# Batch 0 of linear attention and a low-rank mixer: q's tail used last, A on 32 rows, the second heads' k.v amid the normalisations

## The chip, the cores and the metric

One core of a Trainium2 chip runs the whole program. The metric is device time in microseconds (us) of one execution. Seven runs of the kernel before gave a median of 320.61 us (319.73 to 321.92).

## The reference

Eight batches; each has q, k and v with 8 heads of 576 rows by 64. Attention is linear: relu, each row weighted once by a cosine and once by a sine of its position, and no softmax.

```python
def phi(x, c, s):
    r = np.maximum(x, 0.0)
    return np.concatenate([r * c, r * s], axis=-1)
q_p, k_p = phi(q, cos_w, sin_w), phi(k, cos_w, sin_w)
kv = np.einsum('bhsf,bhsd->bhfd', k_p, v)
z = np.sum(k_p, axis=2)
num = np.einsum('bhsf,bhfd->bhsd', q_p, kv)
den = np.einsum('bhsf,bhf->bhs', q_p, z)[..., None] + 1e-06
x = num / den                        # heads side by side: 576 x 512 per batch
h = x.transpose(0, 2, 1) @ U @ V     # U: 576 x 32, V: 32 x 576
u = x + h.transpose(0, 2, 1)
out = u + np.maximum(u @ w_ch1, 0.0) @ w_ch2   # 512 -> 2048 -> 512
```

## The kernel before

**Tiling.** A batch's 576 rows are four blocks of 128 rows ("main", loaded as one 1 MB transfer) and a tail of 64 (one transfer of 128 KB in pieces of 256 bytes). The tails of two batches share a tile of 128 rows: batch 0 has rows 0 to 63 of it, batch 1 rows 64 to 127. All products are in bf16 with sums in f32.

**Stages of a batch.** `q_prep`, `k_prep` and `v_prep`/`v_block` turn loads into bf16 tiles (relu times cosine on VectorE, times sine on ScalarE, a cast for v, which has a column of ones beside each head so that k.v also yields z). `qtr_unit` transposes a block of q on TensorE and has VectorE or ScalarE copy it to `q_pT`, or to `q_tlT` for the tail. `kv_unit` is k.v for four heads (20 products, L271), `den_unit` the 20 products for the denominators (L330) with two VectorE operations for the reciprocals (L322, L323), `xh_unit` four products per block (L347) and their normalisation on VectorE (L351). `A_unit` (L392) makes A = U^T x, 32 by 512. `uTd_open` writes x transposed into PSUM (L444), `uTd_mm` adds A and V to it (L458), and `uTd_evac` copies it as uT. `u_unit` (L409) makes u untransposed. `g1_main` is the hidden layer (4 products of 512 columns for each of 16 blocks, L493, and a relu on ScalarE, L502), `g2_part` the output layer (L545).

**A in four parts.** In the kernel before, the five blocks of rows in `A_unit` go to four column groups of 32 (`lo = c % 4 * R`): blocks 0 to 3 each to its own, the tail on top of group 0. A thus stands as four partial sums on 128 rows, and V is needed four times one below the other. `V_four` makes this `V_bf` out of the loaded `V_32` with two products against four identities (L199, L203), and `V_evac` copies it on ScalarE.

**Order of the work.** The instructions of each engine run in the order in which the Python code calls them (`manual_schedule`); the framework adds the waits. PSUM tiles are drawn from rotating sets named X, T (one buffer each), o (two) and g (three), so an operation can also wait for the reader of an older tile. For batches 2 to 7 a plan places attention beside the hidden layer of earlier batches. Batches 0 and 1 are written out by hand. Batch 0 has nothing beside it: `keep_warm` puts filler products (L179) on TensorE. After the front (q blocks, their transposes, k blocks; L706 to L715) `chain_head(0)` takes v's first heads, k.v of heads 0 to 3, their denominators and normalisations, and k.v of heads 4 to 7 after the fourth block. `chain_mid(0)` does the other four heads, opens two of the four transposed blocks, makes the first half of A and closes the two blocks; `chain_end(0)` makes the second half of A and opens the other two blocks. Then `g1_main` of batch 0 starts, with batch 1's transposes between its blocks. Batch 1 runs through `chain_head(1)`, `chain_mid(1)` and `chain_end(1)` in the same way, with `g1_main` of batch 0 as filling.

**Loads.** SP issues the loads of q, k and v (`load_main` L75, `load_tail` L81) in program order, for batch 0: q, q tail, k, k tail, v tail, v's first four heads, v's other heads; then V and U, then batch 1. qst, qt, vst and vt have one buffer each, so that a load of batch 1 waits for the readers of batch 0. GpSimd issues the weights: the first block of w1 (`w1_load(0)`, 512 columns) behind a copy that waits for batch 0's k tail (L717), the second behind its cast of V, the other two behind batch 1's transposed q tail (L755), w2 later.

Of the kernel before, what the change touches and what calls it, by code (L numbers as in the profile page):

```python
# [17 lines left out]
def kernel(  # L18
# [58 lines left out]
            in_=src[b, h0:h1, 0:512, :].rearrange("h (p c) d -> p h (c d)", c=4),  # L77
        )

    def load_tail(dst, src, b, eng=None):  # L80
        (eng or nc.sync).dma_start(  # L81
            out=dst[tail(b), :, :],
            in_=src[b, :, 512:S, :].rearrange("h s d -> s h d"),
        )

    w1_bf = const.tile([P, 4, DH], BF16)
# [37 lines left out]
            allow_small_or_imprecise_dtypes=True,  # L124
        )
    load_main(qst[0], q, 0)
    load_tail(qt[0], q, 0)
    load_main(kst[0], k, 0)
    load_tail(kt[0], k, 0)
    load_tail(vt[0], v, 0)  # L130
    load_main(vst[0], v, 0, 0, 4)
    load_main(vst[0], v, 0, 4, 8)
    nc.sync.dma_start(out=stV, in_=moe_V)
    nc.sync.dma_start(
# [250 lines left out]
    def A_unit(b, tag, bufs, eng=None, n0=0, n1=DM, a_ps=None):  # L385
        if b not in A_sb:
            A_sb[b] = pool.tile([P, DM], BF16, tag="A_sb", bufs=2, name="A_sb")
        if a_ps is None:
            a_ps = ps.tile([P, DM], FP32, tag=tag, bufs=bufs, name="a_ps")
        for c in range(5):  # L390
            lo = c % 4 * R
            nc.tensor.matmul(  # L392
                out=a_ps[lo : lo + R, n0:n1],
                lhsT=U_of(b, c),
                rhs=x_of(b, c)[:, n0:n1],
                start=(c < 4),
                stop=(c > 0),
            )
        cast(eng or V_, A_sb[b][:, n0:n1], a_ps[:, n0:n1])
        return a_ps  # L400

    def u_unit(b, c, tag, bufs):
        if b not in u_bf:
            u_bf[b] = pool.tile([P, 4, DM], BF16, tag="u_bf", bufs=3, name="u_bf")
            if b % 2 == 0:
                u_tl[b // 2] = pool.tile([P, DM], BF16, tag="u_tl", bufs=2, name="u_tl")
        rows = slice(0, P) if c < 4 else tail(b)
        va = ps.tile([P, DM], FP32, tag=tag, bufs=bufs, name="va_ps")
        nc.tensor.matmul(out=va, lhsT=V_bf[:, c, :], rhs=A_sb[b], start=True, stop=True)  # L409
        nc.vector.tensor_tensor(  # L410
            out=u_bf[b][:, c, :] if c < 4 else u_tl[b // 2][rows, :],
            in0=x_of(b, c, rows),
            in1=va[rows, :],
            op=ALU.add,
        )
# [40 lines left out]
    def uTd_mm(b, d):  # L456
        t = uT_ps[b, d]
        nc.tensor.matmul(  # L458
            out=t.rearrange("m c t -> m (c t)"), lhsT=A_sb[b][:, d * P : d * P + P],
            rhs=V_bf[:, 0:4, :].rearrange("r c t -> r (c t)"), start=False, stop=True,  # L460
        )

    def uTt_direct(pr, tag, bufs, eng):
        uTt_alloc(pr)
        t = ps.tile([P, 4, P], FP32, tag=tag, bufs=bufs, name="uTt_ps")
        for d in range(4):
            dd = slice(d * P, d * P + P)
            nc.tensor.matmul(
                out=t[:, d, :], lhsT=x_tl[:, dd], rhs=ident, start=(d == 0), stop=False
            )  # L470
            for i in range(2):
                nc.tensor.matmul(
                    out=t[:, d, tail(i)], lhsT=A_sb[2 * pr + i][:, dd],
                    rhs=V_bf[:, 4, tail(i)], start=False, stop=(d == 3 and i == 1),
                )
        cast(eng, uT_tl[pr], t)

# [93 lines left out]
    def loads(b, eng):  # L571
        def kk():
            alloc_k(b)
            load_tail(kt[b], k, b, eng)
            load_main(kst[b], k, b, eng=eng)

        def vv():
            alloc_v(b)
            load_tail(vt[b], v, b, eng)
            load_main(vst[b], v, b, eng=eng)  # L580

        def qq():
            alloc_q(b)
            load_tail(qt[b], q, b, eng)
            load_main(qst[b], q, b, eng=eng)

        return kk, vv, qq
# [58 lines left out]
    TL = (0, 1, 2, 3, 4)  # L646
    O2, G3 = ("o", 2), ("g", 3)

    def chain_head(b, fill, xt):
        if b == 0:  # L650
            v_prep(b, 0, 4, (4,), (A_,))
            v_block(b, 0, 4, 0, 3, V_)
            v_block(b, 0, 4, 3, 4, A_)
        kv_unit(b, 0, "T", 1)
        fill(0)
        rec0 = den_unit(b, 0, 4, "X", 1)
        if b == 0:
            v_prep(b, 4, 8, (4,), (A_,))
        v_block(b, 4, 8, 0, 4, A_)
        fill(1)  # L660
        for n, c in enumerate(ORD):
            xh_unit(b, c, 0, 4, rec0, *xt[n])
            if n == 1:
                fill(2)
            if n == 3:
                kv_unit(b, 1, "T", 1, A_)
        if b == 0:
            V_four("X", 1)
            V_evac(A_)

    def chain_mid(b, fill, xt, dt):
        fill(3)
        m = 3 if b == 0 else 2
        rec1 = den_unit(b, 4, 8, *dt)
        if b == 1:

            nc.sync.dma_start(out=mark2, in_=rec1[0:1, 0, 0:1])
        for n, c in enumerate(ORD[:m]):
            xh_unit(b, c, 4, 8, rec1, *xt[n])
        u01 = ps.tile([P, 2, 512], FP32, tag="X", bufs=1, name="u01")  # L680
        uTd_open(b, 0, None, None, u01[:, 0, :].rearrange("p (c t) -> p c t", c=4))
        uTd_open(b, 1, None, None, u01[:, 1, :].rearrange("p (c t) -> p c t", c=4))
        a0 = A_unit(b, "T", 1, A_, 0, 256)
        for n in (m, m + 1):
            xh_unit(b, ORD[n], 4, 8, rec1, *xt[n])
        fill(4)
        uTd_mm(b, 0)
        uTd_mm(b, 1)
        uTd_evac(b, 0, A_)
        uTd_evac(b, 1, V_ if b == 0 else A_)  # L690
        for n in range(m + 2, 5):
            xh_unit(b, ORD[n], 4, 8, rec1, *xt[n])
        fill(5)
        return a0

    def chain_end(b, a0):
        A_unit(b, "T", 1, V_, 256, 512, a0)
        uTd_open(b, 2, "o", 2)
        uTd_open(b, 3, "o", 2)

    def warm0(n):
        m = (2, 1, 0, 1, 1, 2)[n]
        if m:
            keep_warm(m, *(O2 if n == 0 else G3))

# [54 lines left out]
    st1 = {}  # L760
# [7 lines left out]
    xt1 = (O2, O2, O2, O2, O2)  # L768
    at(7, lambda: keep_warm(2, "X", 1))
    at(7, lambda: chain_head(1, fill1, xt1))  # L770
    at(7, lambda: st1.update(a=chain_mid(1, fill1, xt1, ("T", 1))))
    at(7, lambda: chain_end(1, st1["a"]))
    at(13, lambda: uTd_close(1, 2, V_), lambda: uTd_close(1, 3, A_))

    slots, todo = [], {}
# [59 lines left out]
```

## Time and profile before

| | |
|---|---|
| median of 7 runs | 320.61 us (319.73 to 321.92) |
| the profiled execution: its time, its span from first to last instruction | 321.55 us, 319.6 us |
| TensorE busy | 311.8 us, 98% of the span |
| VectorE, ScalarE, GpSimd busy | 154.2, 150.4, 34.8 us |
| mean granted clock of TensorE | 0.995 |
| moved by DMA | 51.90 MB, 162 GB/s over the span |
| filler products (L179) | 42, 12.9 us |
| first hidden product of batch 0 (L493) | starts at 22.58 us |
| k.v of batch 1 in full flow (L271) | from 35.28 us |

All times within the execution are counted from the start of the span. A row of a timeline gives start and length, engine, line, operation, output and inputs, the number of instructions merged into the row, and in brackets how long the engine had been idle before it and what ended that. PE is TensorE, PEld its weight loads, ACT ScalarE, DVE VectorE, POOL GpSimd, SP the engine that issues loads. A busy TensorE is not always doing useful work: in the first 22 us much of it is filler. A row's start is the safe reading; a product is shown with its whole pipeline time, so that rows of TensorE overlap.

### The profile page before, as it was taken

Reading aid. Unit: us, or ns where it says so; the run is one execution under the profiler, and the core shown is the slowest. Engines: PE = TensorE matmul, PEld = TensorE weight load, DVE = VectorE, ACT = ScalarE, POOL = GpSimd, SP = SyncE. Lnnn points to the kernel's source line nnn. Section 1 sums busy time; section 2 is a strip of 40 time slices with the busy share of each in tenths; the row PEclk is TensorE's granted clock in tenths of the full one; section 3 lists DMA queues with packets and bytes.
Section 4 is the critical chain, followed back from the end, with each engine's and each line's share of the span. In section 5 each row is a group of like instructions: output and inputs, shape, how many; then the busy total and the mean of one; then the engine's idle time right before and its main releaser. Section 6 shows DMA issues by size and latency. Waiting matters only on the chain.

```text
span 319.6 us, 5781 instructions
## 1 busy us (share of the span) xinstructions
PE 311.8 (98%) x2386; PEld 162.8 (51%) x2386; DVE 154.2 (48%) x341; ACT 150.4 (47%) x251; POOL 34.8 (11%) x71
## 2 busy tenths in 40 slices
PE   8899799999999999999999999999999999999996
PEld 3565464475545544475455444565454444464443
DVE  5777653762777646036926585154836520001211
ACT  3857655585904256658500077558400166750000
POOL 2232500200120140000211100000121100000000
PEclk9999799999999999999999999999999999999999
DMA  7999999987198937990799859930692140001122
GB/s 216 297 259 267 209 211 299 281 236 238 36 202 164 292 101 141 227 281 12 163 197 284 279 116 180 295 120 21 134 211 71 60 98 0 2 0 68 66 83 81
DMA packets 83755, 51.90 MB, mean 162 GB/s; under 512 B 51890, under 2 KB 80946, under 8 KB 83730
## 3 DMA queue, kind: packets, MB, share of 16 engines
q1 hardware_dynamic: 77154, 40.21, 52.7%
q0 software_dynamic: 6432, 11.27, 14.6%
q8 instruction: 18, 0.29, 0.4%
q10 hardware_dynamic: 144, 0.07, 0.1%
q14 instruction: 7, 0.06, 0.1%
HBM read 36.86 MB, written 9.44 MB: 145 GB/s over the span
## 4 chain that ended last, share of the span: by engine, by line
PE 87%; DMA 7%; SPq 2%; ACT 1%; DVE 1%; issue 0%; DVEq 0%
PE o_ps L545 39%; PE g_ps L493 33%; DMA kt<-in_k_dram 5%; PE gt_ps L513 4%; PE kv_ps L271 3%; PE va_ps L409 3%; PE x_ps L365 3%; DMA vst<-in_v_dram 2%; SPq L81 1%; PE a_ps L392 1%; ACT k_p L237 1%; PE t_ps L288 1%; SPq L75 1%; ACT hid L502 0%; PE xh_ps L347 0%
## 5 line engine op out<-in xcount | busy, mean ns | idle before, releaser
L502 ACT ACTIVATE hid<-g_ps 128x512 bf16<-128x512 f32 x128 | 76.3, 597 | 102.4 <-PE g_ps L493 101.9
L493 PE MATMUL g_ps<-uT,w_bf 128*128 128x512 bf16 x512 | 119.7, 382 | 0.4 <-DMA w_bf<-in_moe_w_ch_dram 0.4
L545 PE MATMUL o_ps<-w_bf,hid 128*128 128x512 bf16 (+2 forms) x528 | 119.2, 373 | 0.0
L493 PEld LDWEIGHTS <-w_bf 128*128 128x128 bf16 x512 | 49.0, 98 | 56.9 <-issue 1.4
L545 PEld LDWEIGHTS <-hid 128*128 128x128 bf16 x528 | 48.7, 98 | 52.8 <-issue 1.7
L555 DVE TENSOR_TENSOR o_sb<-u_bf,o_ps 128x512 f32<-128x512 bf16 (+2 forms) x33 | 22.1, 670 | 62.7 <-PE o_ps L545 62.6
L565 POOL DMA_DIRECT2D out_dram<-o_sb x24 | 13.5, 563 | 164.4 <-DVE o_sb L555 154.4
L410 DVE TENSOR_TENSOR u_bf<-x_bf,va_ps 128x512 bf16<-128x512 bf16 x32 | 21.8, 687 | 10.1 <-PE va_ps L409 10.1
L105 DVE CAST kv<-kv_ps 128x260 bf16<-128x260 f32 x14 | 6.0, 429 | 32.2 <-PE kv_ps L271 32.2
L237 ACT ACTIVATE q_p<-qst,sinw 128x512 bf16<-128x512 f32 x22 | 15.1, 713 | 4.7 <-DMA qst<-in_q_dram 4.7
L375 DVE TENSOR_TENSOR x_bf<-x_ps,rec 128x512 bf16<-128x512 f32 x24 | 16.6, 691 | 0.8
L513 PE MATMUL gt_ps<-uT_tl,w_bf 128*128 128x128 bf16 x256 | 15.6, 219 | 0.0
L409 PE MATMUL va_ps<-A_sb,V_bf 128*128 128x512 bf16 x40 | 15.2, 379 | 0.0
L545 PE MATMUL o_ps<-w_bf,hid_tl 128*128 128x512 bf16 x64 | 15.1, 379 | 0.0
L513 PEld LDWEIGHTS <-w_bf 128*128 128x128 bf16 x256 | 14.6, 98 | 0.5
L322 DVE TENSOR_SCALAR rec<-x_ps 128x8 f32<-128x8 f32 (+1 forms) x30 | 5.0, 165 | 20.2 <-PE x_ps L365 20.1
L179 PE MATMUL w_ps<-zero 128*128 128x512 bf16 x42 | 12.9, 442 | 1.8 <-DVE halfpi L142 1.2
L271 PEld LDWEIGHTS <-k_p 128*128 128x128 bf16 x256 | 11.3, 97 | 5.5 <-ACT k_p L237 2.0
L271 PE MATMUL kv_ps<-v_ext,k_p 128*128 128x65 bf16 x256 | 12.2, 193 | 1.5 <-ACT k_p L237 0.8
L239 DVE TENSOR_SCALAR k_p<-kst,cosw 128x512 bf16<-128x512 f32 x27 | 13.0, 499 | 0.0
L103 ACT ACTIVATE v_ext<-vst 128x512 bf16<-128x512 f32 (+2 forms) x19 | 12.3, 661 | 0.9 <-DMA vst<-in_v_dram 0.8
L520 ACT ACTIVATE hid_tl<-gt_ps 128x512 bf16<-128x512 f32 x16 | 9.4, 598 | 5.5 <-PE gt_ps L513 5.5
(105 smaller groups left out, 249.7 us busy)
## 6 DMA issues: line engine op xcount, KB each, us to landing
qst<-in_q_dram SPq DMA_DIRECT2D x8, 1024.0 KB, 10.4
kst<-in_k_dram SPq DMA_DIRECT2D x8, 1024.0 KB, 7.8
vst<-in_v_dram SPq DMA_DIRECT2D x6, 1024.0 KB, 10.3
out_dram<-o_sb POOLq DMA_DIRECT2D x24, 256.0 KB, 4.5
w_bf<-in_moe_w_ch_dram POOLq DMA_DIRECT2D x8, 512.0 KB, 10.8
vst<-in_v_dram SPq DMA_DIRECT2D x4, 512.0 KB, 8.3
out_dram<-o_sb SPq DMA_DIRECT2D x7, 256.0 KB, 2.3
qt<-in_q_dram SPq DMA_DIRECT2D x8, 128.0 KB, 9.2
```

The source lines that it names most:

```text
L237: nc.scalar.activation(out=o, in_=i, func=AF.Relu, bias=0.0, scale=w)
L239: eng.tensor_scalar(out=o, in0=i, scalar1=0.0, scalar2=w, op0=ALU.max, op1=ALU.mult)
L271: nc.tensor.matmul(out=acc[:, i, :], lhsT=k_p[b][:, c, h, :] if c < 4 else k_tl[:, h, :], rhs=vx[:, c, h, :], start=(c == 0), stop=(c == 4),)
L375: nc.vector.tensor_tensor(out=x_of(b, c, rows).rearrange("p (g i d) -> p g i d", g=2, d=D), in0=view[:, :, :, 0:D], in1=rec[rows].unsqueez ...
L409: nc.tensor.matmul(out=va, lhsT=V_bf[:, c, :], rhs=A_sb[b], start=True, stop=True)
L410: nc.vector.tensor_tensor(out=u_bf[b][:, c, :] if c < 4 else u_tl[b // 2][rows, :], in0=x_of(b, c, rows), in1=va[rows, :], op=ALU.add,)
L493: nc.tensor.matmul(out=g_ps.rearrange("p (c t) -> p c t", c=4), lhsT=w1_bf[:, d, j * P : j * P + P], rhs=uT[b][:, :, d, :], start=(d == 0) ...
L502: nc.scalar.activation(out=hid[b][:, j, :], in_=g_ps, func=AF.Relu, bias=0.0, scale=1.0)
L513: nc.tensor.matmul(out=g_ps[:, jj, :], lhsT=w1_bf[:, d, j * P : j * P + P], rhs=uT_tl[pr][:, d, :], start=(d == 0), stop=(d == 3),)
L545: nc.tensor.matmul(out=o[:, cols], lhsT=lhs[:, j, c * P : c * P + P], rhs=w2_bf[:, j, cols], start=(j == 0), stop=(j == NJ - 1),)
L555: nc.vector.tensor_tensor(out=o_sb[:, cols], in0=u[:, cols], in1=o[:, cols], op=ALU.add)
L565: eng.dma_start(out=out[b, 0:512, cols].rearrange("(p c) n -> p c n", c=4)[:, c, :], in_=o_sb[:, cols],)
```

## The change

It concerns batch 0 and, by moved names alone, batch 1, whose calls keep their order.

- **Loads.** q's tail of batch 0 is issued behind k, its tail, the first four heads of v's tail (a transfer of its own now) and the first half of v. The rest of v's tail follows it, then v's second half. There is one transfer more.
- **q's tail used last.** `q_prep` and `qtr_unit` of the tail stand after v's first casts, and around the first k.v, instead of before k. The blocks are normalised in the order 0, 1, 2, 3, tail.
- **Second heads' k.v** comes after the second block of the first normalisations instead of the fourth, and the first denominators are now called after the casts of v's second heads.
- **A on 32 rows.** For batch 0 all five products add up in one group of 32 rows, A's copies take 32 rows, and whatever uses A of batch 0 takes `V_32`. `V_four` and `V_evac` stay for the other batches.
- **Around A.** For batch 0 the first half of A goes ahead of the opening of the first two transposed blocks, and ScalarE copies both. The denominators of the second heads use the set T.
- **Fillers.** Five products of `keep_warm` fewer.
- The loads of batch 1 are written down behind the whole of batch 0's chain; SP issues them in the same order as before.

```diff
@@ -77,10 +77,10 @@
             in_=src[b, h0:h1, 0:512, :].rearrange("h (p c) d -> p h (c d)", c=4),
         )
 
-    def load_tail(dst, src, b, eng=None):
+    def load_tail(dst, src, b, h0=0, h1=H, eng=None):
         (eng or nc.sync).dma_start(
-            out=dst[tail(b), :, :],
-            in_=src[b, :, 512:S, :].rearrange("h s d -> s h d"),
+            out=dst[tail(b), h0:h1, :],
+            in_=src[b, h0:h1, 512:S, :].rearrange("h s d -> s h d"),
         )
 
     w1_bf = const.tile([P, 4, DH], BF16)
@@ -124,11 +124,12 @@
             allow_small_or_imprecise_dtypes=True,
         )
     load_main(qst[0], q, 0)
-    load_tail(qt[0], q, 0)
     load_main(kst[0], k, 0)
     load_tail(kt[0], k, 0)
-    load_tail(vt[0], v, 0)
+    load_tail(vt[0], v, 0, 0, 4)
     load_main(vst[0], v, 0, 0, 4)
+    load_tail(qt[0], q, 0)
+    load_tail(vt[0], v, 0, 4, 8)
     load_main(vst[0], v, 0, 4, 8)
     nc.sync.dma_start(out=stV, in_=moe_V)
     nc.sync.dma_start(
@@ -388,16 +389,25 @@
         if a_ps is None:
             a_ps = ps.tile([P, DM], FP32, tag=tag, bufs=bufs, name="a_ps")
         for c in range(5):
-            lo = c % 4 * R
+            lo = c % 4 * R if b > 0 else 0
             nc.tensor.matmul(
                 out=a_ps[lo : lo + R, n0:n1],
                 lhsT=U_of(b, c),
                 rhs=x_of(b, c)[:, n0:n1],
-                start=(c < 4),
-                stop=(c > 0),
-            )
-        cast(eng or V_, A_sb[b][:, n0:n1], a_ps[:, n0:n1])
+                start=(c < 4) if b > 0 else (c == 0),
+                stop=(c > 0) if b > 0 else (c == 4),
+            )
+        rows = slice(0, P) if b > 0 else slice(0, R)
+        cast(eng or V_, A_sb[b][rows, n0:n1], a_ps[rows, n0:n1])
         return a_ps
+
+
+
+    def A_of(b, cols=slice(0, DM)):
+        return A_sb[b][:, cols] if b > 0 else A_sb[b][0:R, cols]
+
+    def V_of(b):
+        return V_bf if b > 0 else V_32
 
     def u_unit(b, c, tag, bufs):
         if b not in u_bf:
@@ -406,7 +416,7 @@
                 u_tl[b // 2] = pool.tile([P, DM], BF16, tag="u_tl", bufs=2, name="u_tl")
         rows = slice(0, P) if c < 4 else tail(b)
         va = ps.tile([P, DM], FP32, tag=tag, bufs=bufs, name="va_ps")
-        nc.tensor.matmul(out=va, lhsT=V_bf[:, c, :], rhs=A_sb[b], start=True, stop=True)
+        nc.tensor.matmul(out=va, lhsT=V_of(b)[:, c, :], rhs=A_of(b), start=True, stop=True)
         nc.vector.tensor_tensor(
             out=u_bf[b][:, c, :] if c < 4 else u_tl[b // 2][rows, :],
             in0=x_of(b, c, rows),
@@ -456,8 +466,8 @@
     def uTd_mm(b, d):
         t = uT_ps[b, d]
         nc.tensor.matmul(
-            out=t.rearrange("m c t -> m (c t)"), lhsT=A_sb[b][:, d * P : d * P + P],
-            rhs=V_bf[:, 0:4, :].rearrange("r c t -> r (c t)"), start=False, stop=True,
+            out=t.rearrange("m c t -> m (c t)"), lhsT=A_of(b, slice(d * P, d * P + P)),
+            rhs=V_of(b)[:, 0:4, :].rearrange("r c t -> r (c t)"), start=False, stop=True,
         )
 
     def uTt_direct(pr, tag, bufs, eng):
...
@@ -646,69 +656,84 @@
     TL = (0, 1, 2, 3, 4)
     O2, G3 = ("o", 2), ("g", 3)
 
-    def chain_head(b, fill, xt):
-        if b == 0:
-            v_prep(b, 0, 4, (4,), (A_,))
-            v_block(b, 0, 4, 0, 3, V_)
-            v_block(b, 0, 4, 3, 4, A_)
-        kv_unit(b, 0, "T", 1)
-        fill(0)
-        rec0 = den_unit(b, 0, 4, "X", 1)
-        if b == 0:
-            v_prep(b, 4, 8, (4,), (A_,))
-        v_block(b, 4, 8, 0, 4, A_)
-        fill(1)
-        for n, c in enumerate(ORD):
-            xh_unit(b, c, 0, 4, rec0, *xt[n])
-            if n == 1:
-                fill(2)
-            if n == 3:
-                kv_unit(b, 1, "T", 1, A_)
-        if b == 0:
-            V_four("X", 1)
-            V_evac(A_)
-
-    def chain_mid(b, fill, xt, dt):
-        fill(3)
-        m = 3 if b == 0 else 2
-        rec1 = den_unit(b, 4, 8, *dt)
-        if b == 1:
-
-            nc.sync.dma_start(out=mark2, in_=rec1[0:1, 0, 0:1])
-        for n, c in enumerate(ORD[:m]):
-            xh_unit(b, c, 4, 8, rec1, *xt[n])
+    def chain_begin(b):
         u01 = ps.tile([P, 2, 512], FP32, tag="X", bufs=1, name="u01")
-        uTd_open(b, 0, None, None, u01[:, 0, :].rearrange("p (c t) -> p c t", c=4))
-        uTd_open(b, 1, None, None, u01[:, 1, :].rearrange("p (c t) -> p c t", c=4))
-        a0 = A_unit(b, "T", 1, A_, 0, 256)
-        for n in (m, m + 1):
-            xh_unit(b, ORD[n], 4, 8, rec1, *xt[n])
-        fill(4)
-        uTd_mm(b, 0)
-        uTd_mm(b, 1)
-        uTd_evac(b, 0, A_)
-        uTd_evac(b, 1, V_ if b == 0 else A_)
-        for n in range(m + 2, 5):
-            xh_unit(b, ORD[n], 4, 8, rec1, *xt[n])
-        fill(5)
-        return a0
+        for d in (0, 1):
+            uTd_open(b, d, None, None, u01[:, d, :].rearrange("p (c t) -> p c t", c=4))
 
     def chain_end(b, a0):
         A_unit(b, "T", 1, V_, 256, 512, a0)
         uTd_open(b, 2, "o", 2)
         uTd_open(b, 3, "o", 2)
 
-    def warm0(n):
-        m = (2, 1, 0, 1, 1, 2)[n]
-        if m:
-            keep_warm(m, *(O2 if n == 0 else G3))
+    def chain0():
+        v_prep(0, 0, 4, (4,), (A_,))
+        v_block(0, 0, 4, 0, 3, V_)
+        v_block(0, 0, 4, 3, 4, A_)
+        q_prep(0, 4, (V_, A_))
+        kv_unit(0, 0, "T", 1)
+        qtr_unit(0, 4, 0, H, V_, *G3)
+        v_prep(0, 4, 8, (4,), (A_,))
+        v_block(0, 4, 8, 0, 4, A_)
+        rec0 = den_unit(0, 0, 4, "X", 1)
+        for n, c in enumerate(TL):
+            xh_unit(0, c, 0, 4, rec0, *(O2, O2, G3, G3, G3)[n])
+            if n == 1:
+                kv_unit(0, 1, "T", 1, A_)
+        V_four("X", 1)
+        V_evac(A_)
+        rec1 = den_unit(0, 4, 8, "T", 1)
+        for n, c in enumerate(TL[:3]):
+            xh_unit(0, c, 4, 8, rec1, *(O2, O2, G3)[n])
+        a0 = A_unit(0, "T", 1, A_, 0, 256)
+        chain_begin(0)
+        for n, c in enumerate(TL[3:]):
+            xh_unit(0, c, 4, 8, rec1, *G3)
+        keep_warm(1, "o", 2)
+        uTd_mm(0, 0)
+        uTd_mm(0, 1)
+        uTd_evac(0, 0, A_)
+        uTd_evac(0, 1, A_)
+        keep_warm(1, "o", 2)
+        return a0
+
+    def chain1(fill):
+        kv_unit(1, 0, "T", 1)
+        fill(0)
+        rec0 = den_unit(1, 0, 4, "X", 1)
+        v_block(1, 4, 8, 0, 4, A_)
+        fill(1)
+        for n, c in enumerate(ORD):
+            xh_unit(1, c, 0, 4, rec0, *O2)
+            if n == 1:
+                fill(2)
+            if n == 3:
+                kv_unit(1, 1, "T", 1, A_)
+        fill(3)
+        rec1 = den_unit(1, 4, 8, "T", 1)
+
+        nc.sync.dma_start(out=mark2, in_=rec1[0:1, 0, 0:1])
+        for n, c in enumerate(ORD[:2]):
+            xh_unit(1, c, 4, 8, rec1, *O2)
+        chain_begin(1)
+        a0 = A_unit(1, "T", 1, A_, 0, 256)
+        for c in ORD[2:4]:
+            xh_unit(1, c, 4, 8, rec1, *O2)
+        fill(4)
+        uTd_mm(1, 0)
+        uTd_mm(1, 1)
+        uTd_evac(1, 0, A_)
+        uTd_evac(1, 1, A_)
+        xh_unit(1, ORD[4], 4, 8, rec1, *O2)
+        fill(5)
+        chain_end(1, a0)
 
     keep_warm(18, "X", 1)
-    for c in TL:
+    for c in TL[:4]:
         q_prep(0, c, (V_, V_ if c == 3 else A_))
-    for n, c in enumerate(TL):
-        qtr_unit(0, c, 0, H, (V_, A_, V_, A_, V_)[n], *(G3 if n < 3 else O2))
-        if n in (1, 3):
+    for c in TL[:4]:
+        qtr_unit(0, c, 0, H, (V_, A_, V_, A_)[c], *(G3 if c < 3 else O2))
+        if c in (1, 3):
             keep_warm(1, "X", 1)
     for c in TL:
         k_prep(0, c, (V_, V_ if c == 3 else A_))
@@ -717,7 +742,7 @@
     G_.tensor_copy(out=mark, in_=kt[0][0:TS, 0, 0:1])
     w1_load(0)
     cast_uv()
-    chain_head(0, warm0, (O2, O2, G3, G3, O2))
+    a0 = chain0()
     alloc_q(1)
     load_main(qst[1], q, 1)
     load_tail(qt[1], q, 1)
@@ -728,7 +753,6 @@
     load_tail(vt[1], v, 1)
     load_main(vst[1], v, 1, 0, 4)
     load_main(vst[1], v, 1, 4, 8)
-    a0 = chain_mid(0, warm0, (O2, G3, O2, G3, O2), G3)
     for c in (0, 1):
         q_prep(1, c, (None, A_))
     chain_end(0, a0)
```

`chain1` is `chain_head`, `chain_mid` and `chain_end` of batch 1 written out as one, with the same calls in the same order.

More of the change, by code (lines that the diff above doesn't have):

```diff
@@ L472, in uTt_direct @@
                 nc.tensor.matmul(
-                    out=t[:, d, tail(i)], lhsT=A_sb[2 * pr + i][:, dd],
-                    rhs=V_bf[:, 4, tail(i)], start=False, stop=(d == 3 and i == 1),
+                    out=t[:, d, tail(i)], lhsT=A_of(2 * pr + i, dd),
+                    rhs=V_of(2 * pr + i)[:, 4, tail(i)], start=False, stop=(d == 3 and i == 1),
                 )
@@ L573, in kk @@
             alloc_k(b)
-            load_tail(kt[b], k, b, eng)
+            load_tail(kt[b], k, b, eng=eng)
             load_main(kst[b], k, b, eng=eng)
@@ L578, in vv @@
             alloc_v(b)
-            load_tail(vt[b], v, b, eng)
+            load_tail(vt[b], v, b, eng=eng)
             load_main(vst[b], v, b, eng=eng)
@@ L583, in qq @@
             alloc_q(b)
-            load_tail(qt[b], q, b, eng)
+            load_tail(qt[b], q, b, eng=eng)
             load_main(qst[b], q, b, eng=eng)
@@ L759 @@
     at(6, lambda: [w2_load(n) for n in range(4)])
-    st1 = {}
     def fill1(n):
@@ L766, in fill1 @@
             g1_main(0, 7 + n)
-    xt1 = (O2, O2, O2, O2, O2)
     at(7, lambda: keep_warm(2, "X", 1))
-    at(7, lambda: chain_head(1, fill1, xt1))
-    at(7, lambda: st1.update(a=chain_mid(1, fill1, xt1, ("T", 1))))
-    at(7, lambda: chain_end(1, st1["a"]))
+    at(7, lambda: chain1(fill1))
     at(13, lambda: uTd_close(1, 2, V_), lambda: uTd_close(1, 3, A_))
```

## The prediction

> **What bounds the kernel now.** I read the chain that ended last first, from the start to 46 us. Columns: start, length (both us), what was on the chain.
>
> ```profile
> 7.50 7.66 DMA vst<-in_v_dram
> 15.16 0.02 issue
> 15.18 15.62 DMA kt<-in_k_dram
> 30.80 0.02 issue
> 30.82 0.05 ACT k_tl L237
> ...
> 32.19 1.33 ACT k_p L237 x2
> 33.52 0.48 ACT hid L502
> 34.00 1.23 ACT k_p L237 x2
> 35.24 0.05 issue
> 35.28 0.70 PE kv_ps L271 x17
> ```
>
> From 0.7 to 30.8 us no engine is on this chain: SP issues loads, the second half of batch 0's v lands (15.16), then batch 1's k tail lands (30.80). Batch 0's own arithmetic, which the change rearranges, is not on it. From 30.8 ScalarE prepares k of batch 1, and at 35.28 TensorE begins batch 1's k.v. After that TensorE is the chain: in the stages table it is busy 276.52 of 279.80 us from 39.8 to the end. The end therefore moves with 35.28, and with the work and clock behind it.
>
> Next I read TensorE's timeline for its waits between batch 0's first hidden products and 35.28 (start, length, then idle time and releaser in brackets).
>
> ```profile
> 22.58 0.60 PE L493 MATMUL g_ps<-uT,w_bf 128*128 128x512 bf16 x2 [0.36 <-DMA w_bf<-in_moe_w_ch_dram]
> ...
> 25.77 0.62 PE L288 MATMUL t_ps<-ident,q_tl 128*128 128x128 bf16 x8 [0.43 <-ACT q_tl L237]
> ...
> 34.01 0.29 PE L271 MATMUL kv_ps<-v_ext,k_p 128*128 128x65 bf16 x2 [0.65 <-POOL v_ext L105]
> 34.67 0.20 PE L271 MATMUL kv_ps<-v_ext,k_p 128*128 128x65 bf16 x1 [0.37 <-ACT k_p L237]
> 35.28 0.20 PE L271 MATMUL kv_ps<-v_ext,k_p 128*128 128x65 bf16 x1 [0.41 <-ACT k_p L237]
> ```
>
> TensorE is early three times: for the first block of w1, for q's tail of batch 1, for v and k of batch 1. Behind the second wait stands a load, as ScalarE's timeline shows, and so at 30.82:
>
> ```profile
> 25.00 0.72 ACT L237 ACTIVATE q_tl<-qt,sinw 64x512 bf16<-64x512 f32 x1 [0.75 <-DMA qt<-in_q_dram]
> ...
> 30.82 0.72 ACT L237 ACTIVATE k_tl<-kt,sinw 64x512 bf16<-64x512 f32 x1 [0.74 <-DMA kt<-in_k_dram]
> ```
>
> Last the stages (busy us of each engine, granted clock, DMA share, GB/s):
>
> ```profile
> 17.00:21.00 4.00, 4.00 (x77) 2.65 (x73) 3.57 (x12) 1.53 (x4) 1.49 (x5) 1.00 1.18 234
> 22.70:26.11 3.41, 2.98 (x18) 1.32 (x17) 1.77 (x4) 2.35 (x5) 0.00 (x0) 1.00 1.16 252
> 32.94:36.36 3.42, 1.82 (x23) 0.92 (x22) 2.29 (x6) 3.42 (x6) 3.42 (x5) 1.00 1.24 209
> 36.36:39.77 3.41, 3.28 (x34) 1.82 (x34) 1.72 (x6) 0.92 (x2) 0.52 (x1) 0.50 1.23 200
> ```
>
> The DMA engines are full throughout. At 17 to 21, where w1's first block runs beside q of batch 1, they move 234 GB/s; at 12 to 16, with loads alone, 323. And after the wait at 33.4 to 35.3, TensorE runs 3.41 us at half clock, which costs 3.41 / 2 = 1.7 us.
>
> **The change, part by part** (minus is earlier).
>
> *q's tail leaves the front.* Ahead of k's preparation go ScalarE's q_tl (0.71 us at 8.47), VectorE's q_tl (0.47 at 8.61) and q_tlT (0.42 at 10.43), and TensorE's eight transposes (0.61 at 9.79). ScalarE is last there, and its second q_pT copy still needs the fourth block's transposes (9.6), so it gains 0.35, not 0.71: sin(k) at 10.55 instead of 10.89. One tail takes 0.8 us on the queue (kt lands at 2.71 + 8.6 = 11.3, vt at 4.94 + 7.2 = 12.1). So k and its tail land 0.8 earlier and v's first half, now behind half a v tail, 1.2 earlier (13.5 to 12.3); neither is late. The first k.v goes from 14.11 to about 13.75. The four removed operations come back behind it, and the first denominators wait for them: q_tl on ScalarE to 14.35, transposes to 14.8, copy to 15.25, denominators ready at about 15.6 instead of 15.98. First normalisation: -0.4. Behind q_tl on ScalarE stand the v tail's cast (0.41), moved 0.3 to 0.4 later, and the cast of v's second half; that one waits for a landing at 15.16 anyway (ScalarE idle 0.82 there), so they cost nothing unless q's tail lands after 14.
>
> *Second heads' k.v amid the normalisations.* It needs that cast, 15.18 + 1.08 = 16.26, and this lands no earlier: the same bytes stand ahead of it. So k.v goes from 16.60 to 16.3, and the second denominators from 18.02 to 17.7: -0.3.
>
> *A on 32 rows.* Now four products of A start within 0.12 us of the first (19.43, the fifth at 19.55), on different columns of the array. All five on the same 32 must follow one another. A 128x512 product follows the last after 0.216 us (0.86 for four), so 256 columns take 0.11: five end some 0.3 later per half. That is between 0 (if they are no slower) and 0.54 (five in full); I take 0.3, as both numbers are this trace's. The cast of 32 rows I leave at 0.39, that of 128. Products with 32 rows of A instead of 128 cost the same: v_ps on 32 rows takes 0.38, w_ps on 128 the same. Against this A no longer stands behind the eight opening products (0.53 at 18.90). The fold of V (L199) stays on ScalarE, ahead of A's cast; it was not late (18.59, used at 20.30). Five filler products fewer are 1.1 us of TensorE that lay beside waits. Both transposed blocks copied by ScalarE instead of one by VectorE: 0, they ran one after the other before (VectorE idle 0.55 for ScalarE).
>
> Sum: uT's first two blocks ready at about 21.8 instead of 22.27, -0.2 to -0.8. w1's first block, landed at 11.63 + 10.9 = 22.5, is issued when k's tail lands, so 0.8 earlier. Hidden products begin at about 21.9 instead of 22.58: **-0.65**.
>
> *Where the 0.65 goes.* q of batch 1 lands at 11.95 + 10.0 = 21.95, so ScalarE still does its two q_p until 23.35 and the fourth uT block after it, to 23.9. TensorE waits for that, then for q_tl. That load lands at 12.56 + 12.4 = 25.0, because full DMA engines stand before it, and every byte ahead of it is still ahead of it. The wait of 0.43 becomes about 1.1 us. From 25.77 nothing has moved; k's tail lands at 30.8 by the same count. Even a gain that passed 25.77 would lengthen the 1.43 us of waits ahead of 35.28.
>
> *SP's queue.* In the compiled order each issue on SP waits for the eighth before it to land (before: kst of batch 1 goes at 13.48, v's first half landing at 6.19 + 7.3). One issue more moves that by one. q of batch 1 waits for v's first half, 12.3 instead of 11.95; its tail waits for q_tl of batch 0, 14.35 instead of 12.56; k follows at 15.0 instead of 13.48. All that stands behind them is loads of batch 1. The cover: v's second half, V and U are still in the queue until 15.2 and q's 1 MB after them, and SP was so far ahead that vt's issue hung 6.52 us. Cost between 0 and the full 1.5; I take 0, for no stage from 12 to 30.8 shows a DMA share under 1.1.
>
> *Clock.* The stage 22.70 to 26.11 was busy 2.98 us of 3.41 and stayed warm; one of 1.82 was followed by half clock. With 0.65 more waiting it has about 2.3, between the two. If it cools, 3.4 us at half clock push the hidden product that ScalarE copies at 31.56 to about 32.3, and 35.28 by 0.75; but TensorE then works until 34.9, and the later half clock may go (-1.7). So between -0.95 and +0.75; I take 0, the warm row being as near as the cold one.
>
> The Trainium skill (TensorE: Matmul & The Clock Gate, Part 1) says that the array goes to half rate after at least one idle window of some 3.4 us, counted in fixed windows that do not start with the kernel. The length agrees, 3.41 here; but here a window with 1.82 us of work cooled it, with no idle stretch over 0.65. By the page the added wait could not cool the array and the sum would be 0; by the row it might.
>
> **Sum:** 0 on the profiled execution (span 319.6, 321.55 with what lies around it; the median of the seven runs is 320.61, 0.94 lower). Forecast 320.6 for the median.
>
> **The rivals.**
> *Faster: the half clock goes.* For it: it hangs on how waits fall into windows, and the runs spread from 319.73 to 321.92, more than 1.7. Against: 33.4 to 35.3 is fixed by loads I hold for unmoved. 320.6 - 1.7 = 318.9; if paid for with the early cooling, 319.65.
> *Slower: the loads' queue runs dry.* Place: SP between U's loads and k of batch 1. If q and its tail enter after the queue has emptied (from about 15 us, less the time to first data), every later landing moves, up to 1.5: 35.28 becomes 36.8, 322.1. Against: the DMA share above.
> *The chain is not shortened.* The second half of v lands at 15.16 as before, q's tail takes back what it gave, and hidden products begin at 22.58 still. 320.6 as well; told from the forecast only in the trace.
>
> **How the numbers follow.** The gain is made and absorbed: 0.44. Chain not shortened: 0.09. Half clock goes, or k of batch 1 happens to land a microsecond earlier: 0.27. Queue dry, or cooling without return: 0.20. A measurement of this kernel tells about 0.3% (1 us) from no change. Faster 0.27, same 0.53, slower 0.20. The likeliest case alone holds 319.8 to 321.4; reaching most of the way to 318.9 and 322.1 leaves two in ten out: 319.0 to 321.9.
>
> **What would show it.** Right: the first product of L493's line near 21.9, a wait near 1 us for q_tl at 25.8, k_tl on ScalarE at 30.8, batch 1's first full k.v at 35.3. Wrong: k_tl earlier or later than 30.5 to 31.1, a DMA share under 1 between 12 and 20, or a half clock in another place or none.

## The result and the profile after

The changed kernel takes 324.65 us (median of 14 runs, 322.19 to 329.62); the kernel before, run beside it, 320.80 (33 runs). The ratio is 1.0098, 95% interval 1.0072 to 1.0124: about 3.1 us slower. The ratios in this document leave out executions more than 1.5% above the fastest of the same kernel: two of these 14, three of seven in *change_w1_later*, two of twelve in *before_fewer*, and one each in *qt2*, *four_back_warm* and *padded*. The profiled execution has a span of 323.6 us, against 319.6.

The chain that ended last, in the kernel after (start, length, what):

```profile
5.60 8.50 DMA qt<-in_q_dram
14.10 0.02 issue
...
14.18 0.72 ACT q_tl L238
...
16.27 16.16 DMA kt<-in_k_dram
32.43 0.02 issue
...
36.92 0.70 PE kv_ps L272 x17
```

The tail of q of batch 0 is now on the chain (it lands at 14.10), and the last landing of batch 1's k has gone from 30.80 to 32.43. k.v of batch 1 follows it by the same 4.5 us, at 36.92 instead of 35.28: +1.64 us. Of these, 1.01 us are ScalarE's wait for that landing; the other 0.6 us would have been there without it, as batch 0's hidden products, too, were late. TensorE's timeline of the kernel after, in the stretch in which I expected the gain and its absorption:

```profile
23.27 0.59 PE L503 MATMUL g_ps<-uT,w_bf 128*128 128x512 bf16 x2
...
26.39 0.81 PE L503 MATMUL g_ps<-uT,w_bf 128*128 128x512 bf16 x3 [0.81 <-ACT uT L103]
27.14 0.62 PE L289 MATMUL t_ps<-ident,q_tl 128*128 128x128 bf16 x8
```

There was no gain to absorb: hidden products begin at 23.27, not 21.9, and later than the 22.58 of before.

The other half of the loss is found where I did not look, behind 50 us. First the kernel before, then the kernel after; rows are hidden products (g_ps), the product of A and V for u (va_ps) and the transposed tail of batches 0 and 1 (uTt_ps), and what counts is the distance between starts:

```profile
52.60 0.22 PE L468 MATMUL uTt_ps<-ident,x_tl 128*128 128x128 bf16 x1
...
53.05 1.03 PE L493 MATMUL g_ps<-uT,w_bf 128*128 128x512 bf16 x4
53.92 0.38 PE L409 MATMUL va_ps<-A_sb,V_bf 128*128 128x512 bf16 x1
54.13 1.03 PE L493 MATMUL g_ps<-uT,w_bf 128*128 128x512 bf16 x4
```

```profile
54.72 0.22 PE L478 MATMUL uTt_ps<-ident,x_tl 128*128 128x128 bf16 x1
54.87 0.20 PE L482 MATMUL uTt_ps<-V,A_sb 32*128 32x64 bf16 x1
55.00 0.20 PE L482 MATMUL uTt_ps<-V_bf,A_sb 128*128 128x64 bf16 x1
55.04 0.22 PE L478 MATMUL uTt_ps<-ident,x_tl 128*128 128x128 bf16 x1
...
56.01 1.03 PE L503 MATMUL g_ps<-uT,w_bf 128*128 128x512 bf16 x4
56.97 0.38 PE L419 MATMUL va_ps<-A_sb,V 32*128 32x512 bf16 x1
57.28 1.04 PE L503 MATMUL g_ps<-uT,w_bf 128*128 128x512 bf16 x4
```

Each product lasts what it lasted (0.38 us). But four hidden products and one of A now take 57.28 - 56.01 = 1.27 us, before 54.13 - 53.05 = 1.08. The delay sits before and behind the product with 32 rows, about 0.1 us each: its start is 0.96 us behind that of the four (before 0.87), and the next start 0.31 us behind its own (before 0.21). The transposed tail of the pair of batches 0 and 1, where rows of 32 and 128 alternate, takes 56.01 - 54.72 = 1.29 us, before 53.05 - 52.60 = 0.45.

So the profiled execution adds up: +1.64 up to batch 1's k.v, +0.48 up to the pair's tail (0.2 of it the product of A at 46.49; the rest I put down to the half clock, which now begins at 38.59 and covers denser work), +0.84 in the tail, +0.63 in three products of A: 3.59. The last VectorE result comes at 320.25 instead of 316.68, +3.57.

### The profile page after: what moved, and what is told of

Read it like the earlier page. It is cut to its first block, busy times and chain, and to the rows that moved or that the text cites. A ratio compares the mean times of both kernels' runs of the same rounds, so it can differ in the third digit from the quotient of the medians.

```text
span 323.6 us, 5777 instructions
## 1 busy us (share of the span) xinstructions
PE 313.3 (97%) x2381; PEld 163.0 (50%) x2381; DVE 153.7 (47%) x340; ACT 151.2 (47%) x252; POOL 35.0 (11%) x71
## 4 chain that ended last, share of the span: by engine, by line
PE 87%; DMA 8%; ACT 2%; SPq 2%; DVE 1%; issue 0%; DVEq 0%; ACTq 0%
PE o_ps L555 39%; PE g_ps L503 33%; DMA kt<-in_k_dram 5%; PE gt_ps L523 4%; PE va_ps L419 3%; PE kv_ps L272 3%; DMA qt<-in_q_dram 3%; PE x_ps L366 2%; PE a_ps L393 1%; SPq L81 1%; ACT k_p L238 1%; PE t_ps L289 1%; SPq L75 1%; ACT hid L512 0%; PE xh_ps L348 0%
## 5 line engine op out<-in xcount | busy, mean ns | idle before, releaser
L103 ACT ACTIVATE v_ext<-vst 128x512 bf16<-128x512 f32 (+2 forms) x19 | 12.3, 662 | 2.4 <-DMA vst<-in_v_dram 2.3
L419 PE MATMUL va_ps<-A_sb,V_bf 128*128 128x512 bf16 x35 | 13.3, 379 | 0.0
L240 DVE TENSOR_SCALAR k_p<-kst,cosw 128x512 bf16<-128x512 f32 x27 | 12.9, 495 | 0.2 <-DMA kst<-in_k_dram 0.2
L366 PEld LDWEIGHTS <-q_pT 128*128 128x128 bf16 x192 | 9.1, 98 | 5.5 <-issue 0.6
## 6 DMA issues: line engine op xcount, KB each, us to landing
w_bf<-in_moe_w_ch_dram POOLq DMA_DIRECT2D x8, 512.0 KB, 10.8
```

The costliest lines, as they stand in the source:

```text
L366: nc.tensor.matmul(out=acc[:, g, i * E : i * E + E], lhsT=qT_of(b, c, h), rhs=kv_sb[b][:, h, :], start=True, stop=True,)
L419: nc.tensor.matmul(out=va, lhsT=V_of(b)[:, c, :], rhs=A_of(b), start=True, stop=True)
```

## The experiments

Two theories came out of the traces. **Array:** a change of the number of rows between neighbouring products costs TensorE time. **Loads:** something in the new order of loads makes batch 1's k land later. My rivals to both were the clock (waits and missing fillers let the array cool), and for the loads two different causes. Ratios are to the kernel before on the same chip, with 95% intervals; 0.1% is 0.32 us.

### One part alone, one part undone

*a32_alone*: the kernel before, with the change to `A_unit`, `A_of` and `V_of` alone.

> The kernel before with one part of the change: batch 0's A on 32 rows and V as loaded; loads, order and fillers as before. Theory (array): a product on 32 rows between products on 128 costs TensorE about 0.1 us at each change of rows, since in the trace of the changed kernel the steps of hidden block plus u product went from 1.08 to 1.29 us and the transposed tail of the pair from 0.45 to 1.29. By it k.v of batch 1 still starts at 35.3, the pair's tail takes 1.29, and the time is 1.5 to 1.7 us over before (322.3 to 322.5). Rival (the 32 rows are free, as I predicted, and the loss is all from loads and clock): 320.8 to 321.1.

Ratio 1.0064 (1.0039 to 1.0089), that is 2.05 us, somewhat more than the 1.5 to 1.7 expected. In its trace k's tail is prepared at 30.50, so its loads are not late, and the pair's tail takes 1.28 us. Free it is not.

*four_back*:

```diff
-            lo = c % 4 * R if b > 0 else 0
+            lo = c % 4 * R
...
     def A_of(b, cols=slice(0, DM)):
-        return A_sb[b][:, cols] if b > 0 else A_sb[b][0:R, cols]
+        return A_sb[b][:, cols]
 
     def V_of(b):
-        return V_bf if b > 0 else V_32
+        return V_bf
```

> The changed kernel with batch 0's A back in four parts on 128 rows and V four times, all else as changed. Theory (array): the pair's tail back to 0.45 us, hidden block plus u product to 1.08; k.v of batch 1 still late at 36.9; the time 1.5 to 1.9 us under the changed kernel, about 323. Rival (loads and clock alone): no change, 324.6.

1.0060 (1.0033 to 1.0087): the tail is back at 0.46 us, and 0.6% remain without any 32 rows. All nine executions had a granted clock of 0.995 or less, so the clock is a rival here; it is taken up under the fillers.

*order_back*:

```diff
     load_main(qst[0], q, 0)
+    load_tail(qt[0], q, 0)
     load_main(kst[0], k, 0)
     load_tail(kt[0], k, 0)
-    load_tail(vt[0], v, 0, 0, 4)
+    load_tail(vt[0], v, 0)
     load_main(vst[0], v, 0, 0, 4)
-    load_tail(qt[0], q, 0)
-    load_tail(vt[0], v, 0, 4, 8)
     load_main(vst[0], v, 0, 4, 8)
```

> The changed kernel with batch 0's loads issued in the old order (q tail second, v tail whole), so that one issue fewer stands on SP; q's tail is still used last, so q's tail of batch 1 still waits for it on SP. Theory (loads A: the queue ran dry because q of batch 1 was issued at 13.1 instead of 11.95 and behind the slow tails): q of batch 1 goes at about 12, no stage without loads' traffic around 16, k's tail of batch 1 lands at 30.8 to 31.3, time 1.2 to 1.6 us under the changed kernel. Theory (loads B: it is q's tail of batch 1, held on SP until q_tl of batch 0 is read, with k behind it): k still issued at 15 to 15.6, its tail still lands after 32, no gain.

1.0077 (1.0041 to 1.0114), with the 32 rows still in it. Neither theory had it right: q was issued at 12.98, not at about 12, and yet its bytes flowed without a hole; k of batch 1 was issued at 16.49. Its tail was prepared only at 33.14, but without a wait for its landing: batch 0 had run at half clock, and its first hidden product came at 26.02.

*both_back*: the last two edits together, so that of the change only the order of the chain, q's tail used last and the fewer fillers are left.

> The changed kernel with A back in four parts and the old order of loads: what is left is q's tail used last, the new place of the second heads' k.v, five fillers fewer. Theory (clock): still often cold, 0.7 to 1.5 us above before. Rival (loads): as before, 320.5 to 321.2. If q's tail used last alone did the harm (by holding q's tail of batch 1 on SP), it is above 322 with k issued after 14.5.

1.0004 (0.9985 to 1.0024). Here k of batch 1 is issued at 16.63 and its tail at 17.30, later than in the changed kernel (15.60 and 16.27), and no time is lost. Holding the loads of batch 1 on SP costs nothing. Against four_back, the order of loads is worth 0.56%; against order_back, the 32 rows 0.73%. Each without the other, the two cost 0.60% (four_back) and 0.64% (a32_alone), and the whole change 0.98%; the intervals allow that they add up.

*qt2*: `tag="qt", bufs=1` becomes `bufs=2` in the changed kernel.

> The changed kernel with two buffers for q's tail, so that q's tail of batch 1 no longer waits for the readers of batch 0's tail on SP; all else as changed. Theory (loads A: q of batch 1 itself enters too late): q still issued at 13.1, loads' queue still dry at 16, k's tail of batch 1 lands at 32 or later, gain under 0.4 us. Theory (loads B: the held tail delays k behind it): k issued at about 14, its tail lands at 30.8 to 31.3, 1.2 to 1.6 us under the changed kernel.

1.0102 (1.0054 to 1.0150), no gain: the second sign that q's tail on SP is not the cause. In its trace k is issued at 14.67, almost 1 us earlier than in the changed kernel, and the hole of 15 to 17 us shown below is still there.

### The fillers

*after_warm*, and the same edit on four_back as *four_back_warm*:

```diff
         kv_unit(0, 0, "T", 1)
+        keep_warm(2, "o", 2)
...
             if n == 1:
+                keep_warm(2, "g", 3)
                 kv_unit(0, 1, "T", 1, A_)
...
-    keep_warm(13, "o", 2)
+    keep_warm(19, "o", 2)
```

> The changed kernel with ten filler products more in the waits of batch 0's chain (six more ahead of the first k.v, two behind it, two ahead of the second k.v, where TensorE stood idle for 1.31, 0.52 and 0.60 us). Theory (clock: the waits for q's tail and for v let the array fall to half clock in batch 0, and that is what is lost beyond the 32 rows): granted clock 0.995 to 1.0 in nearly all runs, spread of the runs under 2 us, time about 322.3, that is before plus some 1.6 of the 32 rows. Rival (loads: k's tail of batch 1 lands 1.6 us later and that is the rest): no change in the median, still above 324.

1.0088 (1.0054 to 1.0122): my clock theory fell. The clock was at 0.993 or above in all runs, and the loss stayed. The rival has the loss, but not its place: in this trace k's tail is prepared at 31.02, without waiting for its landing.

> The changed kernel with A back in four parts and the same ten filler products: loads and order of the change, without the 32 rows and without cold stretches. Theory (array and clock together explain all): within 0.3% of before, 320.2 to 321.3, with k's tail of batch 1 landing at 30.5 to 31.5. Rival (loads): still 1.0 to 1.6 us above before, k's tail at 32 or later with the array warm.

1.0051 (1.0021 to 1.0081), as the rival said: loads. k's tail is prepared at 32.41, after a wait for its landing.

*before_fewer*: in the kernel before, `m = (2, 1, 0, 1, 1, 2)[n]` becomes `m = (0, 0, 0, 0, 1, 1)[n]`.

> The kernel before with five of batch 0's seven chain fillers taken away, as many as the change takes; loads, A and order as before. Theory (clock): more runs with granted clock under 1.0 than the 5 in 15 of the kernel before, median 0.5 to 1.5 us above before. Rival (fillers only lie beside waits, as I predicted): no change, 320.5 to 321.2.

0.9991 (0.9962 to 1.0021). Five fillers fewer cost nothing in the ratio. They are not idle, though: the granted clock was under 0.99 in five of the twelve executions, and in none of 26 of the kernel before on the same chip.

### Which load

The DMA view of 15 to 17 us shows the hole. Rows are queues (q1 the loads, q0 the weights) with packets, MB and share of 16 engines; the kernel before first, then the kernel after.

```profile
DMA packets 650, 0.65 MB, mean 327 GB/s; under 512 B 11, under 2 KB 650, under 8 KB 650
...
q1 hardware_dynamic: 631, 0.64, 105.0%
q0 software_dynamic: 19, 0.02, 5.7%
```

```profile
DMA packets 564, 0.43 MB, mean 214 GB/s; under 512 B 132, under 2 KB 558, under 8 KB 564
...
q0 software_dynamic: 347, 0.36, 106.2%
q1 hardware_dynamic: 217, 0.07, 18.4%
```

In the same two microseconds before moves q of batch 1, after moves w1's first block, while the loads' queue moves next to nothing, although q of batch 1 was issued at 13.12. The engines look equally full, over 100% in both; but w1's block fills them at 214 GB/s where the loads reach 327. Only the bytes tell the two apart, not the share. (w1's bytes are counted as they are written, in bf16; the f32 that is read is twice as much.)

*v_whole*: four_back, with `load_tail(vt[0], v, 0)` whole ahead of v's first half, q's tail between the halves.

> A in four parts, the change's order of loads, but v's tail whole ahead of v's first half (so no transfer more, and each issue waits for the same one as before); q's tail still between v's halves. Theory (place: q's tail of small pieces between the halves of v is what lets q of batch 1 start late): loads' queue still empty at 16, 1.2 to 2 us over before. Rival (split: the added transfer, by shifting which landing each issue waits for): queue full at 16, within 0.3% of before.

1.0032 (0.9999 to 1.0065): between theory and rival. q went at 11.56 and w1's block at 10.88, and both shared 15 to 17.

*split_only*: both_back, with v's tail in two transfers, one ahead of each half of v.

> A in four parts, q's tail second as before the change, but v's tail in two transfers, the second between v's halves: one transfer more with q's tail out of it. Theory (place): within 0.3% of before, queue full at 16. Rival (split): 1.2 to 2 us over before, queue empty at 16.

1.0004 (0.9975 to 1.0032): the added transfer is free.

*w1_later*: four_back, and

```diff
-    G_.tensor_copy(out=mark, in_=kt[0][0:TS, 0, 0:1])
+    G_.tensor_copy(out=mark, in_=vst[0][0:TS, 0, 0, 0:1])
     w1_load(0)
```

> A in four parts, the change's order of loads, but w1's first block issued when v's first half has landed (about 13.1) instead of when k's tail has (11.1 to 11.5). Theory (overtaking: w1's first block, issued earlier than its turn, fills the DMA engines at 15 to 17 and q of batch 1 waits behind it; q of batch 1 then lands at 24 instead of 22): q's bytes flow at 15 to 17, time back to within 0.3% of before. Rival (w1 only fills a hole that q of batch 1 leaves by itself): queue empty at 16 all the same, and then nothing moves there; 1.2 us or more over before.

1.0002 (0.9976 to 1.0027). The issue of w1's block moved from 11.2 to 12.9 us, and q of batch 1 flows at 15 to 17 again (first row; 15 to 17 us, loads' queue), and k's tail is prepared at 30.36 (second row, ScalarE's timeline), against 32.45 in four_back (third row):

```profile
q1 hardware_dynamic: 661, 0.66, 109.1%
```

```profile
30.36 0.72 ACT L238 ACTIVATE k_tl<-kt,sinw 64x512 bf16<-64x512 f32 x1 [0.89 <-DMA kt<-in_k_dram]
```

```profile
32.45 0.72 ACT L238 ACTIVATE k_tl<-kt,sinw 64x512 bf16<-64x512 f32 x1 [0.20 <-DMA kt<-in_k_dram]
```

Both wait for the landing itself. Overtaking holds: w1's first block, released by the landing of k's tail, must not be issued well ahead of q of batch 1. Before, the two issues were 0.32 us apart (11.63 and 11.95), in the changed kernel 1.63 (11.49 and 13.12), in v_whole 0.68.

This lead of w1's block sorts all kept traces. With 1.63 to 2.04 us (the changed kernel, four_back, both with fillers, qt2) the loads move 0.07 to 0.15 MB at 15 to 17 us, with 0.68 0.22 MB, and in all others, where w1's block leads by 0.32 at most or comes behind q, 0.57 MB or more. A late q alone does not do it: both_back, order_back and split_only issued q at 12.88 to 13.17 and moved 0.62 to 0.70 MB.

How the hole becomes a late landing is less clear. With it k's tail landed at 31.9 to 32.4, but in after_warm at 30.6, with a hole as deep; without it (kt_first aside, where the tail goes ahead of the blocks) at 29.8 to 31.5, but in change_w1_later at 32.1, in an execution of 326.85 us with much half clock in batch 0.

*kt_first*: the kernel before, batch 1's `load_tail(kt[1], ...)` ahead of `load_main(kst[1], ...)`.

> The kernel before, but batch 1's k tail is loaded ahead of its k blocks instead of behind. ScalarE prepares the tail first, so its 0.72 us should fit in ahead of the landing of the blocks. Theory (the end hangs on the last landing of batch 1's k and ScalarE's row of work behind it): k.v of batch 1 starts 0.5 to 0.8 us earlier, time 0.2 to 0.8 us under before. Rival (v's landing and its cast on GpSimd end as late): no change within 0.1%.

0.9996 (0.9963 to 1.0028): the interval holds both what theory and rival said. Its trace does not decide either: batch 0 ran in part at half clock, and k.v of batch 1 began at 36.98.

### Both causes taken out

*change_w1_later*: the whole change with the w1 edit. *padded*: the same, and A and V of batch 0 on 128 rows, 96 of them zero:

```diff
-    V_32 = const.tile([R, 5, P], BF16)
+    V_32 = const.tile([P, 5, P], BF16)
+    V_.memset(V_32, 0.0)
+    A_sb[0] = pool.tile([P, DM], BF16, tag="A_sb", bufs=2, name="A_sb")
+    V_.memset(A_sb[0], 0.0)
...
-        return A_sb[b][:, cols] if b > 0 else A_sb[b][0:R, cols]
+        return A_sb[b][:, cols] if b > 0 else A_sb[b][:, cols]
```

> The whole change, with w1's first block issued after v's first half has landed. Theory (two causes that add up: 32 rows, and w1's block ahead of q of batch 1): the second is gone, the first is left, 0.5 to 0.75% over before, as with the 32 rows alone (1.0064). Rival (the later w1 block only helped the kernel whose A stood in four parts): still about 1.010.

1.0053 (1.0025 to 1.0082): the second cause gone, the 32 rows' share left.

> As the run beside it, but A and V of batch 0 stand on 128 rows of which 96 are zero, so that no product of A has fewer rows than its neighbours; the five products that make A still follow one another on 32 columns. Theory (array: the cost lies in the change from 128 rows to 32 and back): the pair's tail back to 0.45 us, hidden block plus u product to 1.08, time within 0.3% of before. Rival (the cost lies in making A on one group of columns, five in a row): 0.5% or more over before.

1.0025 (1.0004 to 1.0046). TensorE's timeline of padded, the same stretch as above:

```profile
52.88 0.22 PE L481 MATMUL uTt_ps<-ident,x_tl 128*128 128x128 bf16 x1
52.94 0.19 PE L485 MATMUL uTt_ps<-V,A_sb 128*128 128x64 bf16 x1
52.97 0.19 PE L485 MATMUL uTt_ps<-V_bf,A_sb 128*128 128x64 bf16 x1
...
53.34 2.11 PE L506 MATMUL g_ps<-uT,w_bf 128*128 128x512 bf16 x8
55.28 0.38 PE L422 MATMUL va_ps<-A_sb,V 128*128 128x512 bf16 x1
55.50 1.03 PE L506 MATMUL g_ps<-uT,w_bf 128*128 128x512 bf16 x4
56.36 0.38 PE L422 MATMUL va_ps<-A_sb,V 128*128 128x512 bf16 x1
```

The tail takes 0.46 us, hidden block plus product of A 1.08, as before, with A still made in five products on one column group. So the cost lies in the change of rows: padding alone took the steps back to those of before, while the ratio went from 1.0053 to 1.0025, with intervals that overlap.

What is left in padded, 0.25%, I looked for in the clock of batch 0. Its stages (columns as in the stages of before):

```profile
13.18:16.59 3.41, 2.38 (x56) 2.05 (x56) 1.92 (x5) 2.20 (x6) 1.35 (x2) 1.00 1.12 268
16.59:23.42 6.83, 6.21 (x89) 4.85 (x86) 3.67 (x12) 2.09 (x4) 2.83 (x7) 0.50 1.17 270
```

Half clock from 16.59 to 23.42 puts batch 0's first hidden product at 25.52, and then k's tail is prepared at 32.43 without waiting for its landing. So *padded_warm* got the ten fillers, with w1_later once more beside it:

> The change with w1's first block later, A of batch 0 on 128 rows with 96 zero, and the ten filler products more in batch 0's waits. Both known causes are out. Theory (clock in batch 0: what is left of padded's 0.25% are stretches at half clock in batch 0, from the waits for q's tail and v): granted clock mostly 0.995 to 1.0, time 320.2 to 321.2, at or under before. Rival (the rest is not the clock): 0.2 to 0.4% over before, as padded.

> The same kernel as w1_later (A in four parts, the change's loads, w1's first block after v's first half), beside the one with fillers on the same chip: 1.000 to 1.002 of before, with a half clock in batch 0 in most runs.

padded_warm 1.0010 (0.9959 to 1.0061), the second w1_later 0.9978 (0.9931 to 1.0025), with a granted clock of 1.0 in four of six executions and not the half clock expected in most. Neither differs clearly from before, nor from padded: whether those 0.25% are the clock stays open. Nothing here beats the kernel before beyond its interval.

## Why the prediction was wrong, step by step

**Products with 32 rows cost the same.** The step that failed most: I put the 32 rows at nothing, and alone they cost 2.05 us (a32_alone). I compared the lengths of single products, 0.38 and 0.38, and they are equal; the price lies between products. It was to be seen in the trace of before: the second product of V's fold, on 32 rows, has 128 columns, and the filler behind it, on 128 rows, starts 0.15 us later, where a transpose of 128 columns is followed after 0.056 (eight in 0.45, from 25.77 to 26.23).

```profile
17.64 0.21 PE L203 MATMUL v_ps<-V,four 32*128 32x128 bf16 x1
17.79 0.39 PE L179 MATMUL w_ps<-zero 128*128 128x512 bf16 x1
```

The Trainium skill has the rule (TensorEngine Tiling (Array Packing), Tiling Modes, Key Properties): a change of the tiling mode drains TensorE. It gives no duration, and I had not weighed it; here it is about 0.1 us per change, which makes 0.2 + 0.84 + 0.63 = 1.67 us in the profiled execution of the changed kernel.

**w1's first block 0.8 earlier, a gain.** It was issued 0.14 us earlier by the clock, but 1.63 ahead of q of batch 1. My own numbers had the lead: w1's block at 11.63 - 0.8 = 10.8, q at 12.3 (in fact 13.12). I never set them side by side, since I counted the bytes ahead of a landing and took their order for indifferent. With w1's block later again the loss of the loads, 0.60% or 1.9 us (four_back), is gone (w1_later). Why the landing moves by as much as 1.6 us I can't fully say. By 17 us the changed kernel had moved 4.07 MB against 4.44, by 20 us 5.03 against 5.16, as before still had w1's block to move, and by 28 us, with w1's first two blocks through in both, 7.07 against 7.25. Those 0.18 MB are an estimated 0.7 us at the 249 GB/s that the loads reached at 28 to 31 in before. The rest stays open; the landing of v's second half, with the same loads ahead of it, varied from 15.2 (before) to 17.0 us (kt_first) between executions.

**SP's queue, cost 0, and the slower rival.** The rival had the place (the loads' queue runs dry at 15 us), the size (up to 1.5 us, measured 1.64) and the effect, at a chance of 0.20. That the size fits is luck: its cause, SP's waits, was wrong, as both_back and qt2 show, and its time of 322.1 lacks the 32 rows. And what I held against it, a DMA share above 1.1, is no evidence: the share was 1.25 in the dry stretch (15 to 17 us).

**-0.65 for batch 0.** It became +0.69 in this execution. The first k.v came at 13.68, as worked out (13.75). But q's tail landed at 14.10, not by 14, and v's second half at 16.07, not 15.16, so that the second heads' k.v began at 17.21 instead of 16.3. Making A in five took 0.33 us more per half (0.72 instead of 0.39 from first start to last end), as worked out.

**Where the gain goes.** Not tested by the change, as none arose, nor by both_back (1.0004), whose hidden products begin at 22.82. One execution bears it out, if with a late landing: in v_whole they begin at 21.81, ScalarE still waits 1.27 us for the landing of k's tail, and k.v of batch 1 begins at 36.62. Fillers at nothing: right for the ratio (before_fewer), but not for the clock.

**Clock.** The half clock of 36.36 to 39.77 is there at 38.59 to 42.00. A stretch at half clock in batch 0's chain, which I had not thought of, appears in four_back, order_back, split_only and padded, and in kt_first, without the change. It need not cost its whole length: in split_only and padded it moves k.v of batch 1 to 36.9, but the half clock behind 35 us is then gone, a trade that I had named for a later stage, and both spans are 320.3 us, against 323.6 in the changed kernel with k.v as late (1.67 of these 3.3 us are its 32 rows). It does make single executions long: of the 14 of the changed kernel three had a granted clock of 0.979 or less and took 326.96 to 329.62 us.

## What to carry to other kernels

The price of a product is the distance to the next start: look for the cost of a new operand shape at its neighbours in the trace, not in its own row, and try padding with zeros if the neighbours have more rows. When transfers are reordered, ask of each one that is released by a landing (here the weights) what it will now overtake, and compare bytes moved, since a full DMA share can stand for two thirds of the rate. A chain that is not on the path to the end is no place to pay for speed.

## What the runs showed of the hardware

- w1's blocks, read as f32 and written as bf16 through GpSimd's queue, fill all engines with few bytes: alone, at 16 to 17 us of the changed kernel, they moved 0.20 MB in 1 us. The loads of q, k and v, in packets of 1 KB, reach 327 GB/s in before and 331 in w1_later at 15 to 17. By packets and shares of that stretch, one packet takes an engine an estimated 0.10 us for w1 and 0.05 for the loads.
- Busy time in TensorE's rows does not tell when the array cools: 2.38 us of 3.41 in padded (13.18 to 16.59) was followed by half clock. In the kernel after, the stage of 11.28 to 14.69, one of the steps of 3.41 us counted back from its half clock at 38.59, was busy 1.84, and the clock stayed whole:

```profile
11.28:14.69 3.41, 1.84 (x26) 1.03 (x23) 2.07 (x6) 2.71 (x6) 1.32 (x2) 1.00 1.18 243
14.69:18.11 3.42, 2.41 (x66) 2.24 (x67) 1.96 (x6) 1.69 (x4) 1.62 (x4) 1.00 1.21 232
```
